# Radix 8 in place of radix 4 in a spectral filter that runs beside an MLP on one core

## The chip, the cores and the metric

The kernel runs on one core of a Trainium2 chip. The metric is device time in microseconds (us), of executions that gave the right result. "Span" is the time from the first to the last instruction of one profiled execution; it is 1.7 to 2.9 us shorter than the time of the same execution. TensorE is called PE below (PEld is its weight load), VectorE is DVE, ScalarE is ACT. PSUM is the on-chip memory to which the program has PE write its results, SBUF the one for everything else. The record marks each execution as fast or slow (slow: over 1.5% above the fastest of the same kernel).

## The reference

The input is `x` of 1 x 2048 x 512 in bf16. The output is the sum of the input, a spectral filter of its layernorm, and a gated MLP of its layernorm:

```python
def _A_ref(x, w_r, w_i):                 # w_r, w_i: 2048 x 257
    X = rfft2(x.astype(float32), axes=(-2, -1))
    return irfft2(X * (w_r + 1j * w_i), s=(S, D), axes=(-2, -1)).astype(bfloat16)

def _B_ref(x, w_gate, w_up, w_down):     # 512 x 1792, 512 x 1792, 1792 x 512
    h = gelu(x @ w_gate) * (x @ w_up)
    return h @ w_down

xn = layernorm(A_x)
return A_x + _A_ref(xn, A_w_r, A_w_i) + _B_ref(xn, B_w_gate, B_w_up, B_w_down)
```

## The kernel before

The transform over the 512 channels is a dense matrix multiply (`pd` forward, `fp` back). The transform over the 2048 positions is split: dense matrices do most of it on PE (`cs` forward, `ut` back), and a small transform of radix 4 is done with adds and subtracts on DVE. The MLP has four bands of 512 rows. Each band makes 14 tiles `hT` (the product inside the MLP) and then four `dn` blocks of 14 matmuls, which DVE adds to the input (`bsp`). The recorded texts call the MLP the GLU; a "tally" in them is a sum of DVE operations at their distances from start to start, in the order of DVE's queue.

```python
for c in range(4):                                   # bands
    hT = hpool.tile([P, 14, D], BF16)                # hpool: bufs=2
    for fc in range(14):
        gps = psA.tile([P, D], FP32); ups = psA.tile([P, D], FP32, bufs=3)
        ...                                          # 4 + 4 matmuls of 512 columns
        ...                                          # ACT: sq, gsb, sg; DVE: wtl, z, m1
        tt(out=hT[:, fc, :], in0=m1[:], in1=ups[:], op=ALU.mult)
    for r in range(4):
        dn = psA.tile([P, D], FP32, bufs=1)          # one buffer
        ...                                          # 14 matmuls of hT with wd
        tt(out=bsp[:], in0=xblk[:], in1=dn[:], op=ALU.add)
```

The forward spectral part runs in four quarters `kc`. ACT takes each result out of PSUM, and DVE does the rest on pieces of 128 x 257:

```python
for kc in range(4):
    for r in range(4):
        with hp():                                   # high priority for the scheduler
            cs = p3cs.tile([P, D], FP32, tag="cs")
            for T in range(4):
                b = 4 * T + r
                nc.tensor.matmul(cs[:], lhsT=Fkc[:, 0, b, :], rhs=Pt[:, b, :],
                                 start=(T == 0), stop=(T == 3))
            nc.scalar.copy(out=qq[:, r, 0, 0:257], in_=cs[:, 0:257])
            ...                                      # cs2 in the same way
        ...                                          # two corrections of qq
    ...                                              # radix 4: qq -> bf -> XFk, 16 operations
    for m in range(4):                               # complex multiply by the filter
        tt(out=tm[:, 0, 0:257], in0=xr_, in1=w_r, op=ALU.mult)
        ...                                          # 3 more products, 1 add, 1 subtract
    ...                                              # radix 4 back: XFk -> bi -> YY
```

The way back needs all of `YY`. It is issued with high priority as well:

```python
hpi = hp(); hpi.__enter__()
for rp in range(4):
    for t in range(4):
        ut = p3u.tile([P, D], FP32)
        for kc in range(4):
            ...                                      # 2 matmuls of YY with Rt, 512 columns
        nc.scalar.copy(out=UT[:, rp, t, :], in_=ut[:])
hpi.__exit__(None, None, None)
for c in range(4):
    osb = p4.tile([P, 4, D], BF16)
    for r in range(4):
        ...                                          # fp: 4 matmuls of UT with Ginv
        tt(out=osb[:, r, :], in0=bb[:], in1=fp[:], op=ALU.add)
    nc.sync.dma_start(out=ov[c], in_=osb[:])         # 4 stores of 512 KB
```

A scheduler decides where in each engine's queue these instructions go, from their dependencies and priorities.

## Time and profile before

| | before |
|---|---|
| median of 16 runs | 262.49 us (262.22 to 263.61) |
| span of the profiled run | 260.4 us, PE clock 1.000 |
| PE busy / DVE busy | 239.1 / 183.6 us |
| the 128 `ut` matmuls | in the middle of the MLP, from 187.6 us |
| last `hT` starts | 231.55 us |

The page of the kernel before: busy time and instruction count of each engine, then the span in 40 slices of 6.5 us with the busy share in tenths (9 is 90% or more), then the share of each engine in the chain of waits that ended last.

```profile
PE 239.1 (92%) x1098; PEld 107.4 (41%) x1120; DVE 183.6 (71%) x613; ACT 140.9 (54%) x286; POOL 11.6 (4%) x20
...
PE   0398999999999999999998999999999999989992
...
DVE  3996844448996899997999999995820005872573
...
PE 45%; DVE 36%; ACT 11%; issue 4%; DMA 1%; DVEq 0%; ACTq 0%
```

PE is full nearly everywhere. DVE is full too for much of the way, but it does little or nothing in slices 29 to 33 (counted from 0). The windows of the kernel before (stretch in us, its length, then the busy time of PE, PEld, DVE, ACT and POOL with counts, the PE clock, DMA share and GB/s) show both kinds of stretch:

```profile
core 0: us, PE busy (x) PEld busy (x) DVE busy (x) ACT busy (x) POOL busy (x), PEclk, DMA share, GB/s
87.00:118.00 31.00, 30.42 (x137) 13.09 (x136) 31.00 (x113) 23.86 (x48) 0.00 (x0) 1.00 0.15 50
...
191.00:216.00 25.00, 24.80 (x115) 11.21 (x115) 0.34 (x2) 8.77 (x16) 0.00 (x0) 1.00 0.00 1
```

In the first stretch both engines are full. In the second PE does only `ut`, and DVE, whose inputs come from the MLP's matmuls, has nothing to do. The groups of the kernel before give the cost of the parts that change (line, engine, operation, output and inputs, shape, count, then busy us and mean ns of one, then idle time before them and its releaser):

```profile
L397 PE MATMUL ut<-Rt,YY 128*128 128x512 bf16 x126 | 27.8, 379 | 0.2
...
L286 PE MATMUL cs<-Pt,Fkc 128*128 128x512 bf16 x63 | 18.3, 378 | 0.4 <-ACT cbsb L300 0.3
...
L295 PE MATMUL cs<-Pt,Fkc 128*128 128x512 bf16 x60 | 16.2, 377 | 1.6 <-ACT cbsb L291 1.3
```

The two `cs` groups together and `ut` are 128 matmuls each, some of which the trace misses. The mean of one is its duration, and instructions of a pipelined engine overlap. What counts for a sum is the distance from start to start. The timeline of the kernel before (start, us, engine, line, operation) shows it for DVE: operations that last 0.29 us start 0.20 us apart. It also shows the last `hT` and the last `osb`:

```profile
68.39 0.30 DVE L328 TENSOR_TENSOR tm<-XFk,WRk 128x257 bf16<-128x257 bf16 x1
68.59 0.29 DVE L329 TENSOR_TENSOR tm<-XFk,WIk 128x257 bf16<-128x257 bf16 x1
...
231.55 0.69 DVE L229 TENSOR_TENSOR hT<-m,ups 128x512 bf16<-128x512 bf16 x1
...
256.02 0.69 DVE L419 TENSOR_TENSOR osb<-bsp,fp 128x512 bf16<-128x512 bf16 x1 [0.25 <-PE fp L415]
```

From the end of the last `hT` (232.24) to the end of the span (260.4) there are 28.2 us.

### The profile page before, as it was taken

The numbers are of one execution on the slowest core, as the hardware profiler recorded it, in microseconds if no ns is written. First come the engines' busy times: TensorE is split into PE (matmuls) and PEld (weight loads), VectorE is DVE, ScalarE is ACT, GpSimd is POOL, SyncE is SP. The second block draws the span as 40 slices with busy tenths as digits, with TensorE's granted clock in tenths as the row PEclk, the third lists the DMA queues.
The fourth block names the chain that finished last, engine by engine and source line by source line (L and its number), as shares of the span: only waits on it lengthen the run. The fifth ranks groups of instructions, "written<-read, shape, count | busy, mean of one in ns | idle before, by whom it ended". The sixth has DMA issues, their size and how long they took to land.

```text
span 260.4 us, 3425 instructions
## 1 busy us (share of the span) xinstructions
PE 239.1 (92%) x1098; PEld 107.4 (41%) x1120; DVE 183.6 (71%) x613; ACT 140.9 (54%) x286; POOL 11.6 (4%) x20
## 2 busy tenths in 40 slices
PE   0398999999999999999998999999999999989992
PEld 0354444444444444443444444344444444434441
DVE  3996844448996899997999999995820005872573
ACT  1489977768433587974155799422843336920000
POOL 8520000000000000000000000000000000000000
PEclk9999999999999999999999999999999999999999
DMA  7999930004031503000400000029500000000134
GB/s 262 358 339 372 321 84 1 0 3 161 0 109 36 181 0 81 4 1 20 181 21 23 0 0 0 19 81 386 243 3 0 0 0 1 3 1 0 41 123 161
DMA packets 10242, 23.56 MB, mean 90 GB/s; under 512 B 816, under 2 KB 7088, under 8 KB 9584
## 3 DMA queue, kind: packets, MB, share of 16 engines
q1 hardware_dynamic: 8400, 13.12, 14.8%
q0 software_dynamic: 1824, 10.22, 10.8%
q8 instruction: 9, 0.15, 0.2%
q14 instruction: 9, 0.07, 0.1%
HBM read 21.24 MB, written 2.10 MB: 90 GB/s over the span
## 4 chain that ended last, share of the span: by engine, by line
PE 45%; DVE 36%; ACT 11%; issue 4%; DMA 1%; DVEq 0%; ACTq 0%
PE ut L397 9%; PE gps L203 7%; DVE hT L229 7%; PE ups L209 7%; PE dn L234 6%; DVE z L224 5%; PE fp L415 5%; DVE m L228 4%; PE cs L295 4%; PE pd L264 3%; ACT sg L226 3%; PE cs L286 3%; ACT sq L215 2%; DVE bsp L241 2%; ACT gsb L217 2%
## 5 line engine op out<-in xcount | busy, mean ns | idle before, releaser
L203 PE MATMUL gps<-xnT,wg 128*128 128x512 bf16 x221 | 60.4, 381 | 0.3
L209 PE MATMUL ups<-xnT,wu 128*128 128x512 bf16 x219 | 59.0, 379 | 0.3
L229 DVE TENSOR_TENSOR hT<-m,ups 128x512 bf16<-128x512 bf16 x56 | 38.2, 682 | 27.4 <-PE ups L209 25.2
L234 PE MATMUL dn<-wd,hT 128*128 128x512 bf16 x221 | 53.5, 379 | 2.1 <-DVE hT L229 1.4
L215 ACT ACTIVATE sq<-gps 128x512 bf16<-128x512 f32 x56 | 33.2, 593 | 20.6 <-PE gps L203 20.0
L226 ACT ACTIVATE sg<-z 128x512 bf16<-128x512 bf16 x56 | 35.3, 631 | 15.3 <-DVE z L224 13.9
L234 PEld LDWEIGHTS <-hT 128*128 128x128 bf16 x224 | 21.8, 97 | 30.9 <-DVE hT L229 3.7
L209 PEld LDWEIGHTS <-wu 128*128 128x128 bf16 x224 | 21.9, 98 | 27.1 <-issue 2.0
L217 ACT CAST gsb<-gps 128x512 bf16<-128x512 f32 x56 | 32.6, 581 | 0.0
L203 PEld LDWEIGHTS <-wg 128*128 128x128 bf16 x224 | 21.9, 98 | 25.2 <-issue 0.7
L228 DVE TENSOR_TENSOR m<-sg,gsb 128x512 bf16<-128x512 bf16 x56 | 23.5, 420 | 10.6 <-ACT sg L226 10.5
L397 PE MATMUL ut<-Rt,YY 128*128 128x512 bf16 x126 | 27.8, 379 | 0.2
L224 DVE TENSOR_TENSOR z<-wtl,gsb 128x512 bf16<-128x512 bf16 x56 | 23.5, 420 | 3.6 <-ACT gsb L217 2.9
L219 DVE TENSOR_SCALAR wtl<-sq 128x512 bf16<-128x512 bf16 x56 | 16.0, 287 | 8.1 <-ACT sq L215 8.1
L397 PEld LDWEIGHTS <-YY 128*128 128x128 bf16 x128 | 12.5, 98 | 15.4 <-issue 0.4
L286 PE MATMUL cs<-Pt,Fkc 128*128 128x512 bf16 x63 | 18.3, 378 | 0.4 <-ACT cbsb L300 0.3
L402 ACT CAST UT<-ut 128x512 bf16<-128x512 f32 x16 | 9.3, 584 | 16.2 <-PE ut L397 16.2
L241 DVE TENSOR_TENSOR bsp<-xblk,dn 128x512 bf16<-128x512 bf16 x16 | 10.9, 682 | 9.8 <-PE dn L234 9.8
L189 PE MATMUL tp<-ident,xn 128*128 128x128 bf16 x64 | 7.2, 256 | 11.4 <-DVE xn L183 10.0
L295 PE MATMUL cs<-Pt,Fkc 128*128 128x512 bf16 x60 | 16.2, 377 | 1.6 <-ACT cbsb L291 1.3
L264 PE MATMUL pd<-Gt,xnT 128*128 128x512 bf16 x62 | 16.3, 379 | 0.1
L415 PE MATMUL fp<-Ginv,UT 128*128 128x512 bf16 x62 | 14.8, 378 | 0.4 <-DVE osb L419 0.3
(65 smaller groups left out, 200.2 us busy)
## 6 DMA issues: line engine op xcount, KB each, us to landing
Fkc<-cF SPq DMA_DIRECT2D x4, 1024.0 KB, 4.8
Rt<-cR POOLq DMA_DIRECT2D x1, 4096.0 KB, 13.2
xt<-in_A_x_dram SPq DMA_DIRECT2D x4, 512.0 KB, 5.3
xblk<-in_A_x_dram SPq DMA_DIRECT2D x16, 128.0 KB, 2.9
out_dram<-osb SPq DMA_DIRECT2D x4, 512.0 KB, 2.6
wd<-in_B_w_down_dram POOLq DMA_DIRECT2D x2, 896.0 KB, 15.5
wg<-in_B_w_gate_dram POOLq DMA_DIRECT2D x4, 384.0 KB, 15.7
wu<-in_B_w_up_dram POOLq DMA_DIRECT2D x4, 384.0 KB, 16.1
```

The source lines that it names most:

```text
L203: nc.tensor.matmul(gps[:], lhsT=wg[:, dt, fc * P:(fc + 1) * P], rhs=xnT[:, dt, 4 * c:4 * c + 4, :], start=(dt == 0), stop=(dt == 3),)
L209: nc.tensor.matmul(ups[:], lhsT=wu[:, dt, fc * P:(fc + 1) * P], rhs=xnT[:, dt, 4 * c:4 * c + 4, :], start=(dt == 0), stop=(dt == 3),)
L215: nc.scalar.activation(out=sq[:], in_=gps[:], func=ACT.Square)
L217: nc.scalar.copy(out=gsb[:], in_=gps[:])
L224: tt(out=z[:], in0=wtl[:], in1=gsb[:], op=ALU.mult)
L226: nc.scalar.activation(out=sg[:], in_=z[:], func=ACT.Sigmoid, scale=2.0)
L228: tt(out=m1[:], in0=sg[:], in1=gsb[:], op=ALU.mult)
L229: tt(out=hT[:, fc, :], in0=m1[:], in1=ups[:], op=ALU.mult)
L234: nc.tensor.matmul(dn[:], lhsT=hT[:, fc, r * P:(r + 1) * P], rhs=wd[:, fc, :], start=(fc == 0), stop=(fc == 13),)
L295: nc.tensor.matmul(cs2[:], lhsT=Fkc[:, 1, b, :], rhs=Pt[:, b, :], start=(T == 0), stop=(T == 3),)
L397: nc.tensor.matmul(ut[:], lhsT=lt, rhs=rh, start=(kc == 0 and pi_ == 0), stop=(kc == 3 and pi_ == 1),)
L415: nc.tensor.matmul(fp[:], lhsT=UT[:, r, t, c * P:(c + 1) * P], rhs=Ginv[:, t, :], start=(t == 0), stop=(t == 3),)
```

## The change

The intent: with radix 8 the dense part of the transform over the positions becomes half as large, so PE, the fullest engine, has 27.5 us less to do. The price is more adds on DVE. The forward part now runs in two halves `q` in place of four quarters. The core of the diff:

```diff
+RX = 8
+NQ = 2
...
-    hpool = ctx.enter_context(tc.tile_pool(name="hpool", bufs=2))
+    hpool = ctx.enter_context(tc.tile_pool(name="hpool", bufs=1))
...
-        for kc in range(4):
+        for q in range(NQ):
...
-            for r in range(4):
+            for r in range(RX):
                 with hp():
                     cs = p3cs.tile([P, D], FP32, tag="cs")
-                    for T in range(4):
+                    for T in range(2):
...
-            bf = p3q.tile([P, 2, 4, 258], BF16)
...                                    (radix 4 forward, 16 operations of 257 columns)
+            dft8([(qq[:, n, 0, 0:257], qq[:, n, 1, 0:257]) for n in range(RX)],
+                 [(XFq[:, m, 0, 0:257], XFq[:, m, 1, 0:257]) for m in range(RX)], SC)
...                                    (complex multiply, per m as before, now 8 of them)
+            dft8([(XFq[:, m, 0, 0:257], XFq[:, m, 1, 0:257]) for m in range(RX)],
+                 [(YY[:, q, rp, 0, 0:257], YY[:, q, rp, 1, 0:257]) for rp in range(RX)], SC)
...
-        Rt = p3r.tile([P, 4, 2, 4, D], BF16)
+        Rt = p3r.tile([P, NQ, 2, RX, 256], BF16)
...
-                ut = p3u.tile([P, D], FP32)
-                for kc in range(4):
+                    if t % 2 == 0:
+                        ut = p3u.tile([P, 2, 256], FP32)
+                    for q in range(NQ):
...
-            osb = p4.tile([P, 4, D], BF16)
+            osb = p4.tile([P, RX, D], BF16)
...
-            nc.sync.dma_start(out=ov[c], in_=osb[:])
+            nc.sync.dma_start(out=ov[aT], in_=osb[:])
```

The new `dft8` is written out in 56 operations of 257 columns: two radix-4 butterflies, four adds and four multiplies for the factor 1/sqrt(2), and 16 outputs, for example

```python
cadd(s02r, e[0][0], e[2][0])      # one of 16 in a butterfly: 128 x 257
cadd(outs[0][0], A[0][0], B[0][0])  # one of the 16 outputs
```

So `cs` goes from 128 to 64 matmuls of 512 columns, and `ut` stays at 128 matmuls, of 256 columns in place of 512. The single `hT` buffer makes room: with two, the changed kernel does not fit in SBUF.

## The prediction

> **What bounds it now.** TensorE. The engine table gives PE 239.1 of 260.4 us (92%); the windows show 97-99% from 36 to 216 us. VectorE (DVE) is close behind: 30.0 of 30.0 us in 90:120, 24.8 of 25 in 145:170, but 0.3 of 25 us in 191:216, where the 128 `ut` matmuls run alone in the middle of the GLU. In the timeline 128x512 matmuls start 0.2155 us apart.
>
> **What the change does.** Radix 8 for radix 4.
> - PE: `cs` falls from 128 to 64 matmuls of 512 columns (-13.8 us); the 128 `ut` have 256 columns. Warm 128-column transposes start 0.057 us apart, so I estimate 0.109 for 256 columns (-13.7 us). That is the pace in the Trainium skill, "TensorE: Matmul & The Clock Gate", section "Wait — 56ns, not 53.3ns?" (N / 2.4 GHz + about 2.5 ns); this trace agrees at 128 and 512. PE loses 27.5 us.
> - DVE: 256 spectral tensor-tensors become 336, and 16 scalar multiplies come in. They last 0.289 us but start 0.204 us apart (tensor_scalar 0.135): +18.5 us, not +27. Tallied at such pitches (PSUM-reading ones 0.60, z and m 0.335), DVE work goes from 175 to 193 us, PE work from 235 to 207: nearly equal.
> - Order (built program): `ut` leaves the middle of the GLU and `fp` no longer mixes with the last `dn`. PE now ends with 56 dn, 128 ut, 64 fp; DVE with 4 bsp among about 100 spectral operations, then 16 osb. So ut hides no elementwise work and waits for the DVE tail.
> - One hT buffer for two: the next band's first hT waits for all dn of this band. The order fills this with 15 us of DVE work, against 16 us on PE: I expect under 2 us each.
> - Rt is 2 MB and doesn't wait for DVE. Output goes in two 1 MB stores: the tail, now 3.7 us after the last osb (512 KB lands in 2.6 us, a 1 MB load in 4.8), becomes about 5.9.
>
> **Sum.** Last hT: DVE tally 164.7 us plus idle. Before, the first 14 hT end at 68 us; their tally after is 46.3, so 21.7 us idle, plus a few at the band changes: about 194 us (before, without ut, 207). Then 17 us of DVE work until the first second-half YY is ready, PE idle about 4 us of it; ut 14, fp 14, last osb 1, store 6: 246. Plus 2.4 us between span and time: 248. Of 27.5 us taken off PE, about 15 arrive.
>
> **Predicted: 248 us, range 242 to 255.** Faster by over 2%: 0.93; within 2%: 0.06; slower: 0.01.
>
> **To see in the profile.** PE busy about 213 us, DVE near 200; ut at about 0.11 us pitch in one block after all dn; PE idle 3-6 us before it, released by DVE; the chain of waits mostly on DVE in the GLU, then ut, fp, store; the last store about 6 us; hT waits at the three band changes small.
>
> **What would make it wrong.** ut bound by weight loads[...]; the single hT buffer stalling DVE or PE longer at the band changes; `cs` on one PSUM buffer, now freed twice as often per matmul, stalling PE behind ACT; the idle before ut slowing the PE clock[...]; DVE and PE alternating as bottleneck, so that idle adds up on both.

## The result, and the profile after

| | before | after |
|---|---|---|
| median (runs) | 262.49 us (16) | 249.73 us (8), 248.97 to 250.27 |
| ratio | | 0.9507, interval 0.9491 to 0.9524 |
| span, PE clock | 260.4 us, 1.000 | 247.4 us, 0.981 |
| PE busy / DVE busy | 239.1 / 183.6 us | 217.1 / 199.5 us |

A ratio is the mean time of one kernel's fast runs over that of the other's in the same rounds, so it is not quite the ratio of the medians quoted. The page of the changed kernel, as above and with the row of the PE clock:

```profile
PE 217.1 (88%) x1037; PEld 102.7 (42%) x1056; DVE 199.5 (81%) x709; ACT 138.3 (56%) x286; POOL 11.5 (5%) x20
...
PE   0298999999999999999999999999999775998990
...
DVE  2998665466999999999999899999999989401771
...
PEclk9999999999999999999999999999999799799997
...
PE 56%; DVE 28%; ACT 9%; issue 3%; DMA 2%; DVEq 0%; ACTq 0%
```

The hole in DVE's row in slices 29 to 33 is gone; DVE now pauses in slices 34 to 36, while `ut` runs. PE's row has a new dent in slices 31 to 33, and the clock's row in 31 and 34. The groups of the changed kernel:

```profile
L434 PE MATMUL ut<-Rt,YY 128*128 128x256 bf16 x128 | 16.1, 290 | 3.5 <-DVE YY L395 3.5
...
L352 PE MATMUL cs<-Pt,Fq 128*128 128x512 bf16 x32 | 10.8, 378 | 0.5 <-ACT cbsb L366 0.4
...
L361 PE MATMUL cs<-Pt,Fq 128*128 128x512 bf16 x32 | 9.5, 377 | 0.9 <-ACT cbsb L357 0.4
```

`cs` and `ut` fell as meant; `ut` now waits 3.5 us for the last step of DVE's spectral work. The timeline of the changed kernel from its last `hT` on:

```profile
191.86 0.68 DVE L296 TENSOR_TENSOR hT<-m,ups 128x512 bf16<-128x512 bf16 x1
...
192.60 0.39 PE L302 MATMUL dn<-wd,hT 128*128 128x512 bf16 x1 [1.42 <-DVE hT L296]
...
193.80 4.77 PE L302 MATMUL dn<-wd,hT 128*128 128x512 bf16 x14 [0.81 <-DVE bsp L309]
...
210.79 15.42 PE L434 MATMUL ut<-Rt,YY 128*128 128x256 bf16 x125 [3.50 <-DVE YY L395]
...
226.88 14.56 PE L452 MATMUL fp<-Ginv,UT 128*128 128x512 bf16 x62 [0.67 <-ACT UT L440]
...
241.48 0.69 DVE L456 TENSOR_TENSOR osb<-bsp,fp 128x512 bf16<-128x512 bf16 x1 [0.18 <-PE fp L452]
```

The last `hT` ends at 192.54, which is 39.7 us earlier than before (232.24). Behind it stand 54.9 us (247.4 less 192.54) in place of 28.2, so 26.7 us more. The difference, 13.0 us, is the gain of the span. Before, `ut` stood ahead of the last `hT`; that moves 27.6 us (128 x 0.2155) from the first account to the second. Freed of this move, the first account gained 12.1 us, most of the 13.8 us that `cs` gave up. The second gained 0.9 us, although `ut` itself shrank by 13.7. **The question is therefore where the 13.7 us of `ut` went.**

The windows of the changed kernel show two stretches of the MLP, and then three short ones behind the last `hT`:

```profile
111.00:126.00 15.00, 14.39 (x64) 6.35 (x66) 15.00 (x64) 4.89 (x9) 0.00 (x0) 1.00 0.10 27
169.00:190.00 21.00, 20.87 (x95) 9.29 (x96) 21.00 (x68) 17.98 (x34) 0.00 (x0) 1.00 0.03 7
...
193.80:197.00 3.20, 3.20 (x8) 1.16 (x8) 3.20 (x17) 0.00 (x0) 0.00 (x0) 0.50 0.00 0
206.60:210.80 4.20, 0.70 (x5) 0.21 (x3) 4.20 (x22) 0.00 (x0) 0.00 (x0) 0.99 0.00 0
210.80:214.00 3.20, 3.20 (x16) 2.29 (x17) 2.00 (x23) 0.80 (x2) 0.00 (x0) 0.50 0.01 3
```

In the MLP both PE and DVE are now full, so busy time alone can't say which of them holds the other. Behind the last `hT`, DVE is full until 210.8 but for 1.19 us, while PE waits for about a third of the time, and after each of two gaps PE runs at half its clock for the 3.2 us shown. In the first of the slow stretches it does 8 `dn` matmuls where 3.2 us has room for 15, and in the second 16 `ut` matmuls where it has room for 29.

The Trainium skill ("TensorE: Matmul & The Clock Gate", section "What's actually happening") says that PE's clock is halved when PE was idle for a window of about 3.4 us and comes back after about 3.4 us of work. The trace agrees on the two clocks and on the length of the slow stretch (0.50 from 193.63 to 197.04, which is 3.41 us). But PE was not idle for a whole window before it: before 193.80 it was idle for 1.42 and 0.81 us only, with a matmul between them. What counts as an idle window is worked out below, with the wider operations.

### The profile page after: what moved, and what is told of

It reads as the page before. It is cut to its first block, busy times and chain, and to the rows that moved or that the text cites. A ratio compares the mean times of both kernels' runs of the same rounds, so it can differ in the third digit from the quotient of the medians.

```text
span 247.4 us, 3371 instructions
## 1 busy us (share of the span) xinstructions
PE 217.1 (88%) x1037; PEld 102.7 (42%) x1056; DVE 199.5 (81%) x709; ACT 138.3 (56%) x286; POOL 11.5 (5%) x20
## 4 chain that ended last, share of the span: by engine, by line
PE 56%; DVE 28%; ACT 9%; issue 3%; DMA 2%; DVEq 0%; ACTq 0%
PE ups L276 14%; PE gps L270 13%; PE dn L302 7%; PE ut L434 6%; PE fp L452 6%; PE pd L330 5%; DVE SC L120 4%; DVE SC L123 4%; DVE bsp L309 3%; DVE hT L296 3%; PE cs L361 3%; DVE z L291 2%; DVE m L295 2%; DVE stats L240 2%; ACT sq L282 2%
## 5 line engine op out<-in xcount | busy, mean ns | idle before, releaser
L293 ACT ACTIVATE sg<-z 128x512 bf16<-128x512 bf16 x56 | 35.5, 634 | 14.6 <-DVE z L291 13.2
L456 DVE TENSOR_TENSOR osb<-bsp,fp 128x512 bf16<-128x512 bf16 x16 | 11.0, 688 | 18.3 <-PE fp L452 18.2
L434 PE MATMUL ut<-Rt,YY 128*128 128x256 bf16 x128 | 16.1, 290 | 3.5 <-DVE YY L395 3.5
L256 PE MATMUL tp<-ident,xn 128*128 128x128 bf16 x64 | 7.5, 263 | 11.9 <-DVE xn L250 10.8
L330 PE MATMUL pd<-Gt,xnT 128*128 128x512 bf16 x61 | 17.1, 379 | 0.1
L434 PEld LDWEIGHTS <-YY 128*128 128x128 bf16 x128 | 13.3, 105 | 6.4 <-DVE YY L395 3.7
L240 DVE BATCH_NORM_STATS2 stats<-xt 128x6 f32<-128x512 bf16 x16 | 10.4, 664 | 3.9 <-DMA xt<-in_A_x_dram 3.9
L334 ACT CAST Pt<-pd 128x512 bf16<-128x512 f32 x16 | 9.3, 582 | 5.8 <-PE pd L330 5.8
```

Source lines behind the costliest of these rows:

```text
L293: nc.scalar.activation(out=sg[:], in_=z[:], func=ACT.Sigmoid, scale=2.0)
L330: nc.tensor.matmul(pd[:], lhsT=xnT[:, dt, b, :], rhs=Gt[:, dt, :], start=(dt == 0), stop=(dt == 3),)
L434: nc.tensor.matmul(ut[:, t % 2, :], lhsT=lt, rhs=rh, start=(q == 0 and pi_ == 0), stop=(q == NQ - 1 and pi_ == 1),)
```

## The experiments

Two theories were tested. Some of the expectations call them A and B.

- **A: DVE paces the changed kernel.** Each us of DVE work counts once, wherever it stands; it is what the prediction's tally assumed for the time of the last `hT`.
- **B: PE sets the time of the last `hT`; behind it stands a serial tail.** The tail is whatever DVE still has to do of the second half's spectral work until `YY` is ready (or the `dn` chain, if that is longer), then `ut`, `fp`, `osb` and the store. DVE work counts where it lies in the tail only.

Smaller rivals were the store, the PE clock, the single `hT` buffer, and the place of `ut` in the order. "Gap" is from the start of the last `hT` to the start of the main block of `ut`; "waits" are those of `ut` in the gap.

| run | median us | ratio | last `hT` | `ut` | gap | waits of `ut`, us |
|---|---|---|---|---|---|---|
| the changed kernel | 249.73 | 0.9507 | 191.86 | 210.79 | 18.9 | 3.50 |
| e1_store4 | 248.41 | 0.9451 | 192.10 | 211.12 | 19.0 | 3.50 |
| e2_warm | 247.70 | 0.9420 | 192.51 | 211.08 | 18.6 | filled |
| e4_fused | 242.46 | 0.9228 | 192.00 | 205.69 | 13.7 | none |
| e5_cs128 | 255.48 | 0.9715 | 204.34 | 217.74 | 13.4 | none |
| e6_dvemid | 259.30 | 0.9870 | 191.52 | 219.95 | 28.4 | 11.57 + 2.79 |
| e7_alias | 251.85 | 0.9590 | 190.42 | 213.31 | 22.9 | 5.89 + 2.79 |
| e8_alias_ht2 | 252.98 | 0.9618 | 191.43 | 214.54 | 23.1 | 6.09 + 2.79 |
| e10_fused_dn2 | 243.16 | 0.9251 | 191.34 | 205.96 | 14.6 | 5.39 |
| e11_fused_p300 | 241.31 | 0.9174 | 194.14 | 206.29 | 12.2 | none |

Ratios are against the kernel before; its medians were 262.62, 262.72 and 262.58 us. All outputs were right.

### Four stores in place of two

```diff
-            nc.sync.dma_start(out=ov[aT], in_=osb[:])
+                if rp % 4 == 3:
+                    nc.sync.dma_start(out=ov[aT, :, rp - 3:rp + 1, :], in_=osb[:, rp - 3:rp + 1, :])
```

> Only the output store is split: four stores of 512 KB as in the kernel before, not two of 1 MB. Theory (the last store costs the changed kernel part of its gain): the tail from the last osb to the end shrinks from 5.2 to about 3.7 us, time 248.2 us, 1.5 us less than the changed kernel's 249.7. Rival (store size does not matter, the tail is a fixed latency): no change.

Measured: 248.41 us (0.9451, interval 0.943 to 0.9472), 1.3 us less than the changed kernel. From the end of the last `osb` to the end of the span it took 3.8 us, against 5.2 with 1 MB stores and 3.7 in the kernel before. So the larger store costs about 1.4 us of the tail.

### Work for PE while it waits for YY

```diff
                     if t % 2 == 0:
                         ut = p3u.tile([P, 2, 256], FP32)
+                        if rp == 0 and t == 0:      # once, results overwritten
+                            for k in range(34):
+                                nc.tensor.matmul(ut[:, 0, :], lhsT=YY[:, 0, 0, 0, 0:128],
+                                                 rhs=Rt[:, 0, 0, 0, :], start=True, stop=True)
                     for q in range(NQ):
```

> 34 matmuls whose result is overwritten are put on TensorE ahead of ut, into its 4.2 us of waiting, to keep the clock up. Theory (the wait lets the clock fall, which slows the start of ut): granted clock near 1 in the ut block, its 125 matmuls take 13.7 us and not 15.4, time about 248.0, 1.7 us less. Rival (the slow start of ut is waiting for YY, tile after tile): no change; and if the dummies outlast the wait, slightly slower.

Measured: 247.70 us (245.95 to 248.54), ratio 0.9420 (0.9392 to 0.9449), 2.0 us less. The 128 real `ut` matmuls took 14.28 us from 211.08 on, with the clock at 1.00. So the second slow stretch cost about 1.5 us, and it came from the idle time that the 34 extra matmuls filled. The first slow stretch, now at 195.0 to 198.4 us, stayed.

### The second half's DVE work far earlier

```diff
+            with (tc.high_priority(offset=600) if q == 1 else ExitStack()):
                 ...   # the corrections of qq, both dft8, the multiply, the YY signs
```

> Same instructions; the scheduler is told to rank the elementwise work of the second half (q = 1) 600 places earlier, so the built order has ut inside the last GLU band, fp mixed with the last dn, and no spectral work behind the last hT. Theory (most of the loss is the serial tail: spectral VectorE work, then ut, with TensorE idle): last hT near 208 us, then 28 us as in the kernel before, time about 240 (236 to 244). Rival (the loss is the 18.5 us more of VectorE work or the single hT buffer, wherever it stands): 248 to 251, as that work is unchanged.

Measured: 252.0 us (0.9596, interval 0.9569 to 0.9623), which is slower than the changed kernel. It missed the expectation by 12 us and lies 1 us above what the rival expected (248 to 251), but not for the rival's reason. The timeline of PE in this run shows why:

```profile
175.92 0.38 PE L270 MATMUL gps<-xnT,wg 128*128 128x512 bf16 x1 [4.80 <-ACT gsb L284]
...
180.44 0.59 PE L270 MATMUL gps<-xnT,wg 128*128 128x512 bf16 x2 [0.88 <-ACT gsb L284]
...
184.78 0.59 PE L270 MATMUL gps<-xnT,wg 128*128 128x512 bf16 x2 [2.24 <-ACT gsb L284]
```

The scheduler put some 23 us of spectral work in one bunch at the start of the last band. The MLP's own DVE steps queued behind it, ACT could not go on, and PE starved for 4.80, 0.88 and 2.24 us and some more. Then `ut` came in the middle of the last band, with DVE idle for 10.3 us. The run mixes two effects and so does not test the order of `ut`; the run of the kernel before with `ut` at its end does.

### A dft8 of fewer, wider operations

```diff
-            cadd(s02r, e[0][0], e[2][0])          # 56 operations, most of 257 columns
-            cadd(s02i, e[0][1], e[2][1])
...
+        S4, D4 = sc[:, 0:4, :, 0:257], sc[:, 4:8, :, 0:257]
+        cadd(S4, x[:, 0:4], x[:, 4:8])           # 25 operations, up to 2056 columns
+        csub(D4, x[:, 0:4], x[:, 4:8])
...
```

> The same radix-8 arithmetic with 25 wider VectorE instructions for 56 in each DFT-8: by the tally VectorE does 174.6 us ahead of osb and not 183.6. Theory A (VectorE alone sets the pace to the end of YY): 9 us less, about 240.7. Theory B (to the last hT TensorE sets the pace as well, only the tail behind it is VectorE's alone, which falls from 18.9 to 15.6 us by the tally): last hT stays at 190 to 192.5 us, 3.5 to 5.5 us less, about 245. Rival (wide strided operands run at half the element rate): no gain or slower.

Measured: 242.46 us (242.19 to 243.2), ratio 0.9228 (0.9206 to 0.9251), 7.3 us less. Time alone lies between the two expectations. The timeline of this run decides:

```profile
192.00 0.67 DVE L277 TENSOR_TENSOR hT<-m,ups 128x512 bf16<-128x512 bf16 x1
...
195.54 1.24 DVE L120 TENSOR_TENSOR SC<-XFq 128x2056 bf16<-128x2056 bf16 x1
196.69 1.23 DVE L123 TENSOR_TENSOR SC<-XFq 128x2056 bf16<-128x2056 bf16 x1
...
205.69 14.14 PE L407 MATMUL ut<-Rt,YY 128*128 128x256 bf16 x128
```

DVE has 8.7 us less to do in total (busy 190.8 against 199.5), yet the last `hT` starts at 192.00 and not earlier, against A. The gain is all behind it: `ut` starts 5.1 us earlier, directly behind `dn` with no wait for `YY`, and the clock, not lowered now in either place (0.998 in the mean), gives most of the rest of the profiled execution's gain: from the start of `ut` to `fp` it took 14.8 us in place of 16.1. B's 245 had left the clock out, which is about 1.3 us of the 2.5 that it missed. The size of the clock's part differs between executions: two of the other three had a mean clock of 0.986 and 0.988 and took 242.19 and 243.20 us, no clear difference.

Why did the clock fall at 193.63 in the changed kernel and not here, where the same waits of 1.42 and 0.81 us stand in the same place? In the traces of all 14 kernels the granted clock changes only at multiples of 3.413 us from its first record in that execution. On this fixed grid the windows are, first of the changed kernel and then of this run:

```profile
190.22:193.63 3.41, 1.35 (x6) 0.34 (x5) 3.41 (x13) 0.63 (x1) 0.00 (x0) 1.00 0.01 2
193.63:197.04 3.41, 3.24 (x8) 1.16 (x8) 3.41 (x18) 0.00 (x0) 0.00 (x0) 0.50 0.00 0
...
188.65:192.07 3.42, 2.65 (x13) 0.97 (x10) 3.42 (x13) 1.58 (x3) 0.00 (x0) 1.00 0.01 2
192.07:195.48 3.41, 1.94 (x9) 0.83 (x10) 3.41 (x14) 0.00 (x0) 0.00 (x0) 1.00 0.00 0
```

In the changed kernel both waits fell into one window, in which PE was busy for 1.35 us, and the next window had half the clock. Here the grid lay otherwise: the waits were shared between two windows, busy for 2.65 and 1.94 us, and the clock stayed. It is so throughout: of the 926 windows at full clock in these traces, the 26 with PE busy for at most 1.35 us (40%) were each followed by half the clock, and the 900 with 1.63 us (48%) or more by none. So a short wait costs clock or not by where it falls on the grid, and the grid lies differently in each execution (its first record stood at 14.5 to 18.2 us of the span in these traces).

The operation on 2056 columns starts 1.15 us before the next one; eight of 257 columns would take 1.63 (8 x 0.204). The Trainium skill ("VectorE: DVE Perf Modes", section "The TRN2 errata — SBUF-src ops pay a fixed extra latency per instruction") gives 58 + columns / 2 cycles at 0.96 GHz for such an operation and advises wider tiles. As a distance from start to start this fits: the estimates from it are 194, 328, 596 and 1131 ns for 257, 514, 1028 and 2056 columns, against 204, 335, 600 and 1150 in this run. So wide operands did not run at half the rate, as the rival had it.

### cs done twice

```diff
-                    for T in range(2):            # in both groups, start and stop at the ends
+                    for T in (0, 1, 0, 1):        # start at T == 0, stop at T == 1, as before
```

> The cs half of the change is undone on TensorE alone: each cs group of two matmuls is done twice (the second start overwrites the first, the result is the same), so there are 128 as before, 13.8 us more TensorE work; VectorE work is unchanged. Theory B (TensorE sets the pace up to the last hT, VectorE's tail follows): last hT goes from 192 to about 206 us, the VectorE tail behind it shrinks by some 3 us, so 258 to 262 us. Rival (VectorE alone sets the pace, the cs saving bought nothing): 250 to 252.

The second pass over a group starts the sum afresh, so the result stays right and PE does 64 more matmuls (13.8 us). Measured: 255.48 us (0.9715, interval 0.9676 to 0.9754), 5.75 us more than the changed kernel. The timeline of this run:

```profile
204.34 0.68 DVE L296 TENSOR_TENSOR hT<-m,ups 128x512 bf16<-128x512 bf16 x1
...
217.74 14.14 PE L434 MATMUL ut<-Rt,YY 128*128 128x256 bf16 x128
```

The last `hT` went from 191.86 to 204.34, by 12.5 of the 13.8 us added to PE. So PE does set it, which A did not allow for. But the total rose by less than half of that, between both expectations. DVE used the 12.5 us to do more of its spectral work ahead of the last `hT` (it was busy 173.0 us until then, against 168.8 in the changed kernel): the gap shrank from 18.9 to 13.4 us, `ut` waited for nothing, and the clock did not fall. The gap has a floor, the chain of 56 `dn` matmuls with one PSUM buffer, at about 13.4 us here and 13.7 with the wider operations; it was added to B after this run. As written down, B had the direction right and the size wrong: it had the tail shrink by some 3 us, where the gap shrank by 5.5, and it left out the clock (14.8 us from the start of `ut` to `fp`, in place of 16.1).

### 24 dead adds in the first half

```diff
+            if q == 0:                            # behind the second dft8; results unused
+                for k in range(24):
+                    cadd(SC[:, k % 12, 0, 0:257], SC[:, 12, 0, 0:257], SC[:, 12, 1, 0:257])
```

> 24 dead VectorE additions of 257 columns, 4.9 us by the pitch, are put into the spectral work of the first half, in the middle of the GLU. The built order lets later spectral work slide back, so the tally of VectorE work behind the last hT is 29.7 us and not 18.9. Theory B: last hT stays near 191 to 193 us and the tail takes the 10.8 us: about 260. Theory A (VectorE alone): 4.9 us more, about 254.6. Rival (there is slack on VectorE in the GLU): 250.

Measured: 259.3 us (0.987, interval 0.9846 to 0.9894). A's 254.6 is excluded, B's 260 is close. The timeline of this run:

```profile
191.52 0.67 DVE L296 TENSOR_TENSOR hT<-m,ups 128x512 bf16<-128x512 bf16 x1
...
216.77 0.40 PE L437 MATMUL ut<-Rt,YY 128*128 128x256 bf16 x1 [11.57 <-DVE YY L120]
...
219.95 16.45 PE L437 MATMUL ut<-Rt,YY 128*128 128x256 bf16 x125 [2.79 <-DVE YY L398]
```

The adds are 4.9 us (24 x 0.204), and the time rose by 9.6. The scheduler, which orders by its own estimate, moved further spectral work behind the last `hT`. The windows show it, first of the changed kernel and then of this run, each cut at its last `hT`:

```profile
0.00:191.90 191.90, 175.28 (x805) 78.75 (x821) 168.78 (x593) 128.95 (x270) 11.54 (x20) 1.00 0.28 90
191.90:247.40 55.50, 41.84 (x232) 23.95 (x235) 30.71 (x118) 9.36 (x16) 0.00 (x0) 0.92 0.09 39
```

```profile
0.00:191.60 191.60, 176.58 (x821) 78.79 (x821) 162.27 (x563) 130.02 (x270) 11.64 (x20) 1.00 0.28 90
191.60:257.40 65.80, 41.56 (x235) 24.10 (x235) 41.35 (x171) 9.36 (x16) 0.00 (x0) 0.86 0.08 33
```

Ahead of the last `hT` DVE was busy 6.5 us less (162.27 against 168.78), and the last `hT` came only 0.3 us earlier: DVE does not hold it. Behind it DVE was busy 10.6 us more, and the gap grew by 9.5 us. This run and the previous one together settle theory B against A for this balance of the two engines. They do not say that DVE has much to spare: of the attempts below, the second put 5.2 us more DVE work ahead of its last `hT` than the first (168.73 against 163.53 us busy), and its last `hT` came 2.8 us later.

### Two hT buffers, with a control

Two `hT` buffers fit only if other buffers go. The control makes that room and keeps one `hT` buffer; the other run has the same edit and two.

```diff
-            XFq = p3xf.tile([P, RX, 2, 258], BF16)
+            XFq = qq                              # both runs; also tm and cbsb with bufs=1
...
-    hpool = ctx.enter_context(tc.tile_pool(name="hpool", bufs=1))
+    hpool = ctx.enter_context(tc.tile_pool(name="hpool", bufs=2))   # e8_alias_ht2 only
```

> Control for the next run: the first DFT-8 writes its result back into qq, and tm and cbsb have one buffer, which frees 11 KB a partition. The work is the same, but the built order leaves 23.8 us of VectorE work behind the last hT and not 18.9. Theory B: about 5 us slower than the changed kernel, 254.6. Theory A: 249.7.

> As the control, with two hT buffers, as in the kernel before. The tail by the tally is 23.6 us, like the control's. Theory: the single buffer costs under 2 us at each of three band changes and the spectral work fills them, so within 2 us of the control. Rival (the single hT buffer is what ate the gain): faster than the control by 4 us or more.

Measured: 251.85 us for the control (0.959, interval 0.9557 to 0.9623) and 252.98 with two buffers (0.9618, interval 0.9576 to 0.966). The intervals overlap, and a gain of 4 us from the second buffer is excluded: the rival that the single buffer ate the gain is rejected. The test holds for the control's order of work, as two buffers do not fit in the changed kernel itself. The control itself came out 2.1 us slower than the changed kernel, between the two expectations. Its gap grew by 4.0 us, as B has it, and its last `hT` was 1.4 us earlier, which B did not foresee.

### The kernel before, with ut at its end

```diff
-        hpi = hp()
-        hpi.__enter__()
...
-        hpi.__exit__(None, None, None)
```

> The kernel before (radix 4) with only the high priority of ut taken away, so that the built order has ut behind the GLU, mixed with the last dn, and fp last, as in the changed kernel. YY is ready long before in it. Theory (the order is harmless by itself; what costs is that YY is not ready when TensorE has finished the GLU): within 2 us of the kernel before, 263 to 265. Rival (ut behind the GLU costs by its place): slower by 8 us or more.

Measured: 262.53 us, ratio 0.9992 (0.9967 to 1.0016): no difference. The timeline of this run:

```profile
202.88 0.69 DVE L229 TENSOR_TENSOR hT<-m,ups 128x512 bf16<-128x512 bf16 x1
...
215.73 24.98 PE L395 MATMUL ut<-Rt,YY 128*128 128x512 bf16 x113
...
255.97 0.69 DVE L416 TENSOR_TENSOR osb<-bsp,fp 128x512 bf16<-128x512 bf16 x1 [0.18 <-PE fp L412]
```

`ut` at the end costs nothing by itself, as long as `YY` is ready by then. Here it was: 13 of the `ut` matmuls ran in the pauses between the last `dn` blocks, and the rest followed in one block. (Two records are missing from the trace.)

This run is also the right kernel to compare the changed one with, as both have `ut` at the end. Its last `hT` ends at 203.57, with 56.8 us behind it. Taking off the 13.8 us of `cs` and the 13.7 us of `ut` gives, as an estimate, 189.8 and 43.1, together 232.9. The changed kernel has 192.5 and 54.9. So 2.8 us were lost ahead of the last `hT`, and 11.8 behind it:

| behind the last `hT` | this run, us | with the `ut` in it halved (estimate) | changed kernel, us | lost |
|---|---|---|---|---|
| until the main block of `ut` | 12.2, with 13 `ut` in it | 10.8 | 18.3 | 7.5 |
| main block of `ut`, and `fp`, until the last `osb` | 40.2 | 27.9 | 30.7 | 2.8 |
| last `osb` and store | 4.4 | 4.4 | 5.9 | 1.5 |

In the first row, on PE's side, 1.6 us are the slow `dn` block (4.77 in place of 3.18) and 3.5 the wait for `YY`; the pauses between `dn` blocks, where there is now no `ut` to run, are in it too. What sets the length of this row is DVE, for which `ut` waits at its end: DVE was busy all the way but for 1.19 us, in which it waited for that slow `dn` block. So the slow block can have cost `ut` 1.2 us at most. In the second, about 1.5 are the slow clock (the run with extra matmuls) and 0.7 the wait for `UT`.

### Attempts at a better version

Three runs build on the wider operations, all with four stores and with the last band's `dn` in the two PSUM buffers of `gps`. The second and third also rank the second half's DVE work earlier:

```diff
+            if c == 3:
+                dn = psA.tile([P, D], FP32, tag="gps")
+            else:
                 dn = psA.tile([P, D], FP32, bufs=1)
...
+            with (tc.high_priority(offset=300) if q == 1 else ExitStack()):   # 300, then 450
```

> The fused kernel (242.5), with four stores and with the last band's four dn accumulators in the two free gps banks, so that dn need not wait for bsp. Theory: the stores give 1.3 us, the dn wait is hidden behind the VectorE tail (15.6 us by the tally) and gives under 1 us: 240 to 241.

> As the last, with the second half's VectorE work ranked 300 places earlier, so that by the tally 9.4 us of it stand behind the last hT and not 15.6. Theory B: the last hT stays near 192 us (up to 194: VectorE now has 3 us more than TensorE in the last band), ut follows the last dn about 10 us later and not 13.7: 237 to 240.

> As the last, ranked 450 places earlier: all second-half VectorE work is ahead of the last hT, ut stands in the last GLU band, between its tenth and eleventh column block, and 13 us of spectral work stand bunched in front. Theory: last hT 192 + 14 for ut + some 3 us for the bunch, then about 28 us: 237 to 241. Rival (as in the early-ranked kernel of the first call, the bunch starves TensorE): 244 or more.

The first gave 243.16 us (0.9251, interval 0.9224 to 0.9277) and missed its expectation. Its timeline:

```profile
205.96 16.30 PE L410 MATMUL ut<-Rt,YY 128*128 128x256 bf16 x125 [5.39 <-DVE YY L371]
```

`dn` was done at 200 us, but `YY` was not, so the time won became a wait of 5.39 us, and the clock fell after it. Four stores and a second buffer bought nothing that the wait and the clock did not take back.

The second gave 241.31 us (239.69 to 241.98), ratio 0.9174 (0.9134 to 0.9214), 1.3 us above what was expected. Its timeline shows `ut` with no wait, at full clock, but `dn` waiting for a `bsp` that stood behind spectral work in DVE's queue, and then running at half the clock from 198.58 to 202.00:

```profile
198.58 7.88 PE L286 MATMUL dn<-wd,hT 128*128 128x512 bf16 x27 [2.67 <-DVE bsp L293]
...
206.29 14.14 PE L412 MATMUL ut<-Rt,YY 128*128 128x256 bf16 x128
```

It has the lowest median of all, but its interval overlaps that of the plain wider operations (0.9206 to 0.9251), so it is not clearly better than those. Its fastest execution (239.69 us) is the one with the clock at 1.000 in the mean; the other three, at 0.991 and 0.992, took 241.12 to 241.98.

The third gave 246.05 us (0.936, interval 0.9332 to 0.9388), as its rival expectation had it: the bunch of DVE work starved PE again, with waits of 4.16, 2.30 and 0.78 us, and the last `hT` moved to 215.5, where about 209 was expected.

## Why the prediction was right or wrong

The total of 248 us was right: 249.73, well inside the range. In part this was luck: the first term was near for a reason that does not hold (below), and the terms' errors of -1.5 to +2.1 us largely cancel. Here is the sum that led to it, term by term, with the profiled run beside it:

| term | predicted us | measured us |
|---|---|---|
| last `hT` ends | 194 | 192.5 |
| from there to the main block of `ut` | 17 | 18.3 |
| `ut`, with the wait for the last `UT` | 14 | 16.1 |
| `fp` | 14 | 14.6 |
| last `osb` | 1 | 0.7 |
| store | 6 | 5.2 |
| span | 246 | 247.4 |

- **PE work.** The prediction took off 27.5 us. `ut` copies of 8 matmuls follow each other every 0.873 us when the clock is full, so one is 0.109 us, as estimated. This is again the pace that the Trainium skill gives ("TensorE: Matmul & The Clock Gate", section "Wait — 56ns, not 53.3ns?": columns / 2.4 GHz + about 2.5 ns, an estimate of 0.109 here), so weight loads did not bind `ut`. PE busy is 217.1 where 213 was predicted; the two slow stretches are in it (it is 214.2 with the wider operations, where there are none).
- **DVE work.** Busy 199.5 against "near 200". Counting the adds at the 0.204 us from start to start, and not at their 0.29 us duration, was right.
- **Order and waits.** `ut` in one block behind all `dn`, with a wait of 3.5 us that DVE's `YY` released, is what the prediction said (3 to 6 us). That hiding no elementwise work behind `ut` costs something in itself is not shown; the run of the kernel before with `ut` at the end took the same time.
- **One `hT` buffer.** No cost was found, as predicted, tested with the control. The one PSUM buffer of `cs`, another risk named, did no harm either: PE waited 1.4 us before `cs` (0.5 and 0.9 in the groups), 2.0 in the kernel before.
- **Store.** 5.2 us where 5.9 was predicted, and the run with four stores got 1.4 us of it back.
- **The wrong step.** It is "Last hT: DVE tally 164.7 us plus idle", and with it "the chain of waits mostly on DVE in the GLU". The number it gave was right to 1.5 us, but the reason was not. The chain is 56% PE and 28% DVE, more on PE than before; in the MLP alone, from 36 to 192.5 us, some 93 us of it are on PE and 46 on DVE. Taking DVE work from ahead of the last `hT` did not move it (191.52 with 6.5 us less DVE work, 192.00 with the wider operations), and 13.8 us more of PE work moved it by 12.5. What held the last `hT` was PE's work. The tally came near by luck, because the loads are close: up to the last `hT`, of 191.9 us, PE was busy 175.3 and DVE 168.8.
- **A risk that came true.** The prediction named the idle time before `ut` slowing the PE clock as a thing that could make it wrong, and left it out of the sum. The clock fell twice, before `ut` and before a `dn` block. It is about 1.5 of the 2.1 us by which `ut` was mis-sized, and 1.6 us in the `dn` block, of which at most 1.2 can have reached `ut`.
- **"Of 27.5 us taken off PE, about 15 arrive."** 13.0 us of span and 12.8 of the medians arrived. `cs`'s share arrived for the most part (11 to 12 of 13.8 us), as it shortens the time to the last `hT`. `ut`'s share was nearly all lost behind it: to the DVE work that remained there, to the clock, and to the store.

Still open: the wider operations with four stores and nothing else, which were not run; and a version that spreads the second half's DVE work evenly over the last two bands, in place of one bunch, which was not tried.

## What to carry to other kernels

When two engines are both full, find out which one holds a stretch by adding work to one and taking it from the other, and look at whether the end of that stretch moves; the busy shares and even a tally that gives the right number can't tell. Work that is taken off the fullest engine counts only up to the next thing that must be finished first: here the adds that a larger radix gives to VectorE stood in a serial tail, and writing them as fewer, wider operations gave back another 7.3 us. Moving such work earlier is not free either: in one bunch it starves the engine that it was meant to serve.

## What the Trainium skill lacked or had wrong

- "TensorE: Matmul & The Clock Gate", section "What's actually happening", puts the slow clock down to an idle window of about 3.4 us, and does not say how little work in a window counts as idle. Here windows in which PE was busy for up to 1.35 of 3.41 us (40%) were followed by half the clock, and windows with 1.63 us (48%) or more were not. So waits of 1.42 and 0.81 us were enough in one run, and cost nothing in another, where they fell into two windows.
- "VectorE: DVE Perf Modes", section "The TRN2 errata — SBUF-src ops pay a fixed extra latency per instruction", gives its table without saying whether it means the duration or the distance from start to start, and notes that it is too low for the duration. For bf16 tensor_tensor operations that follow each other it is good as a distance: 194 ns against 204 measured for 257 columns, 1131 against 1150 for 2056; the durations in the trace are 290 and 1240.
- The same page, section "The DRAIN you can't avoid", first says that the next operation does not start until the pipe is empty, and only then that one which is not held starts earlier. Here nearly all spectral operations started 0.204 us after the one before, which lasted 0.29 us, so the second sentence is the one that a sum of DVE work should follow. No run here tests an operation that is held.
